# Position-bias tables in DRAM head by head: a row of 640 columns per head instead of one run per head pair

## The chip, the cores and the metric

The kernel runs on one core of a Trainium2 chip. A core has five engines with a program each: TensorE (PE, matrix products; its weight loads are shown as PEld), VectorE (DVE), ScalarE (ACT), GpSimd (POOL) and SyncE (SP, which here issues nearly all transfers). 16 DMA engines carry the transfers. The metric is the time of one execution on the device in microseconds (us). One execution of each kernel was also recorded by the profiler.

## The reference

Attention over 4 batches, 8 heads, 576 positions, head size 64, with a position bias that a small network computes from two positions, then two feed-forward stages over the 2304 tokens:

```
scores = q @ k.T / sqrt(64) + bias[head]     # bias: 8 heads x 576 x 576
x1     = softmax(scores) @ v                 # heads side by side: 2304 x 512
h      = x1 @ w_in                           # 2304 x 1024
x2     = (layernorm(h * softmax(h)) * g_ln) @ w_out           # 2304 x 512
y      = (sigmoid(x2 @ w_gate) * (x2 @ w_val)) @ w_out2       # inner width 1536
bias[h,i,j] = relu(x[i,j] * w1 + b1) @ w2,   x = log1p(|i-j|) / log1p(max(i,1))
```

The bias is the same for all four batches, so the kernel computes it once for 8 x 576 x 576 and uses it four times.

## The kernel before, in words

**Stages.** Until about 90 us the program computes statistics of the weights and the bias of the first 256 query positions. From there to 545 us run 72 attention ticks (a tick is 128 queries of a head pair of one batch), and between them the rest of the bias, the preparation of the weights of the first feed-forward stage (L706 to L722), and then that stage's tiles (L789 to L854). From 545 to about 655 us the weights of the second feed-forward stage are decoded while the last tiles of the first one run. The rest is the second feed-forward stage.

**One tick.** PE makes the scores of two heads (`a_qk`, L567 to L579). In `a_soft` DVE adds the bias and takes the row maximum (L597, one instruction for each head), ACT prepares the exponent's offset (L602) and takes the exponential (L604). In `a_split` the result becomes two halves of 16 bits (L613 on DVE or L615 on ACT, L616 and L618 on POOL), and SP starts a transposing DMA (L621) whose output `pt` PE multiplies with v (L640).

**The bias tables.** Queries are five tiles: t = 0 to 3 of 128, t = 4 of 64 rows. The tables of t = 0 and 1 are computed in an SBUF buffer (`gkf`), are used there by the first batch pair, and are then rescaled (`rescale0`) and written to the DRAM array `bias_d` by `store0` (L524). For t = 4, 2 and 3, in this order, `bias_grp` computes blocks of 128 key columns for all 8 heads and `bias_out` writes each to `bias_d` (L498 to L507): four blocks c = 0 to 3 of 128 columns, and c = 4 for the last 64 keys. `load_bias` brings the table of a head pair back for a tick: 24 loads of 576 KB (`pair_d`, L548), and 16 of the query tile t = 4 (L545, "M" in the code).

**What a row of `bias_d` holds.** For every query there is a row of 640 columns per head, head after head. The even head of a pair has its 512 first keys and then its last 64; the odd head has its last 64 keys first. So the two heads of a pair are one run of 1152 numbers: 512 keys of the even head, its last 64, the odd head's last 64, and 512 keys of the odd head. For t = 4 the row has the last 64 keys at both ends.

**What sets the order.** The program is built by a scheduler: it takes the instructions as the code records them and decides, by a cost model of its own, in which order each engine gets them. From the end of the attention on PE's order is that of the code. So an instruction more, or a transfer with another form, can change the order of others, far away in the program.

**The weight decode from 545 us on.** `load_pair` (L1079 to L1096) fetches rows of `in_moe2_w_out` into `wraw` (L1090), ACT and DVE unpack them (L191, L192 on ACT, L193, L195 on DVE), ACT sums their squares (L1169), DVE and PE reduce the sums (L162, L164, and L1179 for other matrices), and a scale follows from them. The other two matrices are split into halves by POOL, ACT and DVE (L720 to L722). The first products of the second feed-forward stage are L1404 (into `s_ps`); ACT and DVE take them out of PSUM (L1409, L1410) and form the gated values (L1273, L1274). The last products are L1368 and L1436.

Of the kernel before, what the change touches and what calls it, by code (L numbers as in the profile page):

```python
# [8 lines left out]
F32 = mybir.dt.float32  # L9
# [9 lines left out]
B, H, S, D = 4, 8, 576, 64  # L19
# [83 lines left out]
def attn_moe_kernel(  # L103
# [7 lines left out]
    act, dve, pool, pe, sp = nc.scalar, nc.vector, nc.gpsimd, nc.tensor, nc.sync  # L111
# [7 lines left out]
        return stack.enter_context(tc.tile_pool(name=name, bufs=bufs, **kw))  # L119

    dram = enter(ctx, "scratch", 1, space=DRAM)
    bias_d = dram.tile([5, 128, H, 640], F32, name="bias_d")
    x2_d = dram.tile([18, 128, 4, 2, 128], F16, name="x2_d")

    const = enter(ctx, "const")
# [367 lines left out]
    def bias_out(t, c):  # L493
        gb = bst.pop((t, c))
        np_ = 64 if t == 4 else 128
        if c == 4 and t == 4:
            for o in (0, 576):
                sp.dma_start(out=bias_d[4, 0:64, :, o:o + 64], in_=gb[0:64])  # L498
        elif c == 4:
            sp.dma_start(out=bias_d[t, 0:np_].rearrange("p (a b) n -> p a (b n)", b=2)[:, :, 512:640],  # L500
                         in_=gb[0:np_].rearrange("p (a b) n -> p a (b n)", b=2))
        elif t < 4:
            sp.dma_start(out=bias_d[t, :, :, 128 * c:128 * c + 128], in_=gb)
        else:
            for n in range(2):
                o = 64 + 128 * c + 64 * n
                sp.dma_start(out=bias_d[4, 0:64, :, o:o + 64], in_=gb[64 * n:64 * n + 64, :, 0:64])  # L507


    def pair0(t, hp):  # L510
        return view(gkf, 640 * (4 * hp + t), [[1216, 2], [1, S]])

    def pair_d(t, hp):
        return bias_d[t, :, 2 * hp:2 * hp + 2].rearrange("p h n -> p (h n)")[:, 0:2 * S]

    def rescale0(t, hp):
        g = pair0(t, hp)
# [3 lines left out]
            pool.tensor_scalar(out=g, in0=g, scalar1=col(RT), scalar2=0.0, op0=ALU.mult, op1=ALU.add)  # L521

    def store0(t, hp):
        sp.dma_start(out=pair_d(t, hp).rearrange("p (h n) -> p h n", h=2), in_=pair0(t, hp))  # L524


    brt = {}
# [4 lines left out]
    def load_bias(tk):  # L532
        bp, qd, hp, r, _, bset = tk
# [6 lines left out]
        n = 8 + 2 * (nbr[0] % 4)  # L540
        nbr[0] += 1
        t = gkf[:, 640 * n:640 * n + 2 * S]
        if qd == "M":
            for hh in range(2):
                sp.dma_start(out=t[64 * hh:64 * hh + 64, 0:640], in_=bias_d[4, 0:64, 2 * hp + hh])  # L545
            brt[key] = [t[:, 64:640], t[:, 0:S]]
        else:
            sp.dma_start(out=t, in_=pair_d(2 * qd + r, hp))  # L548
            brt[key] = [t[:, S * hh:S * hh + S] for hh in range(2)]

    trs, glob = {}, {}
# [1004 lines left out]
```

## Time and profile before

| | |
|---|---|
| time, median of 3 runs | 1041.68 us (1038.64 to 1043.49) |
| profiled execution, its own time | 1044.08 us |
| its span in the profile | 1042.3 us |
| mean granted TensorE clock | 0.913 of full speed |
| busy: PE, DVE, ACT, POOL | 898.6, 725.1, 644.3, 390.4 us |
| DMA queue of SP's transfers | 56.5% of the 16 DMA engines' time |

All times in the rows below are in microseconds from the start of the span, unless marked ns. "PE busy (x)" is busy time with the number of instructions. A bracket at the end of a timeline row gives the time that the engine sat idle just before, and what it was released by. A granted clock of 1.00 is TensorE's level of 2.4 GHz, one of 0.50 that of 1.2 GHz; values between are averages over a stretch. A DMA share is the mean busy share of the 16 DMA engines.

### The profile page before, as it was taken

To read this page: it belongs to the slowest core of one execution; us is meant where nothing else is said; L and a number is where in the kernel's file an instruction comes from. 1 tells how busy PE (TensorE), PEld (TensorE's weight loads), DVE (VectorE), ACT (ScalarE), POOL (GpSimd) and SP (SyncE) were. 2 spreads that over 40 slices of the span, in tenths; PEclk is the share of its full clock that TensorE was granted. 3 is DMA by queue.
4 is the path that set the end of the run, shared out by engine and by line. 5 is a ranking of instruction groups with operands and counts; after the bars stand their busy time and mean duration, and the time that the engine had idled before them with its cause. 6 is when DMAs were issued, how large, how long until landed. Compare 5 with 4: busy or idle time off the path is not lost. (4 is left out here: it accounts for less than half of the span.)

```text
span 1042.3 us, 23926 instructions
## 1 busy us (share of the span) xinstructions
PE 898.6 (86%) x9620; PEld 634.8 (61%) x9620; DVE 725.1 (70%) x1487; ACT 644.3 (62%) x1275; POOL 390.4 (37%) x362
## 2 busy tenths in 40 slices
PE   2646665679888789999998989899999999999998
PEld 2634444455666556677775656346668847866873
DVE  6878899776577676667666987659936744771760
ACT  3788886757776888878876888674333322332320
POOL 3257656565666656655650486340000000000000
PEclk9666675769998999999998999899999999999999
DMA  7988999999999899899878444101020010000001
GB/s 222 282 255 205 247 254 246 219 206 189 189 191 198 174 207 179 176 219 207 160 137 310 172 158 171 58 1 61 22 61 1 1 61 21 1 11 31 2 1 41
DMA packets 257360, 144.57 MB, mean 139 GB/s; under 512 B 216417, under 2 KB 231777, under 8 KB 257249
## 3 DMA queue, kind: packets, MB, share of 16 engines
q1 hardware_dynamic: 253952, 139.90, 56.5%
q0 software_dynamic: 2048, 1.58, 0.6%
q8 instruction: 75, 1.23, 0.5%
q10 hardware_dynamic: 1248, 1.57, 0.4%
q14 instruction: 37, 0.30, 0.1%
HBM read 80.36 MB, written 20.19 MB: 96 GB/s over the span
## 5 line engine op out<-in xcount | busy, mean ns | idle before, releaser
L616 POOL TENSOR_TENSOR p<-p,p 128x1024 f16<-128x1024 f32 x72 | 158.0, 2194 | 123.3 <-ACT p L615 86.0
L1292 DVE TENSOR_TENSOR fr<-prod,fr 128x512 f32<-128x512 f32 x126 | 85.1, 688 | 92.3 <-PE prod L1368 90.6
L1436 PE MATMUL ops<-w2f,gv 128*128 128x512 f16 x648 | 142.5, 379 | 0.0
L604 ACT ACTIVATE p<-p,m,sc 128x576 f32<-128x576 f32 x144 | 123.9, 862 | 2.4
L597 DVE CUSTOM_DVE_ANT_0 p<-score,gk 128x576 f32<-128x576 f32 x144 | 102.9, 751 | 11.6 <-PE score L579 7.0
L846 PE MATMUL x2ps<-lt,w1f 128*128 128x128 f16 x1728 | 106.2, 221 | 3.5 <-ACT lt L834 1.9
L1436 PEld LDWEIGHTS <-gv 128*128 128x128 f16 x648 | 63.4, 98 | 73.7
L1404 PE MATMUL s_ps<-xb,w2f 128*128 128x512 f16 (+1 forms) x576 | 101.4, 335 | 3.7 <-DVE acc L162 3.4
L846 PEld LDWEIGHTS <-w1f 128*128 128x128 f16 x1728 | 101.0, 99 | 4.1 <-issue 1.6
L640 PE MATMUL xps<-gk,pt 128*128 128x64 f16 (+1 forms) x2240 | 86.8, 202 | 15.8 <-DMA pt<-p 14.1
L640 PEld LDWEIGHTS <-pt 128*128 128x128 f16 (+1 forms) x2240 | 81.9, 107 | 26.3 <-DMA pt<-p 17.0
L463 PEld LDWEIGHTS <-mask 128*128 128x128 f16 (+1 forms) x1312 | 62.2, 118 | 53.3 <-issue 23.4
L1368 PEld LDWEIGHTS <-w2f 128*128 128x128 f16 x864 | 84.5, 98 | 11.8 <-issue 1.1
L1404 PEld LDWEIGHTS <-w2f 128*128 128x128 f16 x576 | 56.9, 100 | 47.0 <-issue 7.4
L1273 ACT ACTIVATE gv<-fr 128x512 f16<-128x512 f32 (+1 forms) x60 | 34.8, 586 | 81.4 <-DVE fr L1426 70.5
L789 PE MATMUL hps<-w1f,xt 128*128 128x512 f16 x312 | 78.5, 398 | 5.5 <-DVE gk L262 2.6
L463 PE MATMUL bp<-rhs,mask 128*128 128x64 f16 (+1 forms) x960 | 50.0, 220 | 28.6 <-DVE gb L489 11.5
L574 PE MATMUL score<-gk,qt 64*128 64x512 f16 x384 | 59.8, 418 | 15.4 <-DVE m L597 7.0
L1368 PEld LDWEIGHTS <-w2s 128*128 128x128 f16 x648 | 63.4, 98 | 7.3
L789 PEld LDWEIGHTS <-xt 128*128 128x128 f16 x384 | 38.1, 102 | 48.8 <-issue 14.0
L615 ACT ACTIVATE p<-p 128x1152 f16<-128x1152 f32 x54 | 62.4, 1157 | 7.0 <-DMA pt<-p 4.9
L602 ACT ACTIVATE m<-m,sc 128x1 f32<-128x1 f32 x144 | 39.3, 286 | 32.9 <-DVE m L597 32.6
(207 smaller groups left out, 1760.7 us busy)
## 6 DMA issues: line engine op xcount, KB each, us to landing
gk<-bias_d SPq DMA_DIRECT2D x24, 576.0 KB
wraw<-in_moe_w_out_dram SPq DMA_DIRECT2D x20, 512.0 KB
sraw<-in_q_dram SPq DMA_DIRECT2D x12, 384.0 KB
sraw<-in_k_dram SPq DMA_DIRECT2D x12, 384.0 KB
sraw<-in_v_dram SPq DMA_DIRECT2D x12, 384.0 KB
bias_d<-gk SPq DMA_DIRECT2D x8, 576.0 KB
qraw<-in_q_dram SPq DMA_DIRECT2D x64, 64.0 KB
kv<-in_k_dram SPq DMA_DIRECT2D x32, 128.0 KB
```

Source lines behind the costliest of these rows:

```text
L463: pe.matmul(big[0:np_, jj // 8, o:o + 64], lhsT, rhs[i].rearrange("p c h g -> p (c h g)"), start=(i == 0), stop=(i == 1),)
L597: dve.tensor_tensor_reduce(out=pp[:, hh], in0=score[:, 960 * hh:960 * hh + S], in1=bi, scale=1.0, scalar=-3.0e38, op0=ALU.add, op1=ALU.max ...
L604: act.activation(out=pp[:, hh], in_=pp[:, hh], func=ACTF.Exp, bias=m[:, 2 + hh:3 + hh], scale=col(C), accum_out=sm[:, c + hh:c + hh + 1])
L615: act.activation(out=hi, in_=pp, func=ACTF.Copy)
L616: pool.tensor_tensor(out=p16[:, :, 640:1152], in0=view(pp, 0, [[640, 2], [1, 512]]), in1=view(p16, 0, [[1280, 2], [1, 512]]), op=ALU.subtract)
L640: pe.matmul(o, a, b_, start=(n == 0), stop=(n == len(seq) - 1))
L789: pe.matmul(h, xt[:, xl, kk, off:off + 128], win16[:, 2 * kk + n, wl], start=(kk == 0 and xl == 0 and wl == 0), stop=(kk == 3 and xl == 1),)
L846: pe.matmul(ps[:, dc], wout16[:, f, wl, 128 * dc:128 * dc + 128], lt[:, ll, f], start=(n == 0), stop=(n == 23))
L1292: dve.tensor_tensor(out=out_, in0=a, in1=b, op=op)
L1368: pe.matmul(p[:, jf, 0:nn], w(wl, kk, jf), x(xl, kk), start=(m == 0), stop=(m == 5))
L1404: pe.matmul(ps[:, 0:n], w[:, 4 * (j // 4) + c, wl, o:o + 128], xx[:, 0:n, c, xl, :], start=(m == 0), stop=(m == 11))
L1436: pe.matmul(ps, gvs[j // 4][:, gl, j % 4, 128 * tt:128 * tt + 128], w2h16[2][:, j, wl], start=(m == 0), stop=(m == 35))
```

## The change

`bias_d` becomes an array with the head ahead of the query: 128 rows of 640 columns for each head, one after the other. The row of every head, even or odd, and of every query tile, now has its last 64 keys at both ends: 64, then 512, then 64. An even head is read from column 64 on, an odd head from column 0 on, 576 columns each.

```
-    bias_d = dram.tile([5, 128, H, 640], F32, name="bias_d")
+    bias_d = dram.tile([5, H, 128, 640], F32, name="bias_d")
...
         elif c == 4:
-            sp.dma_start(out=bias_d[t, 0:np_].rearrange("p (a b) n -> p a (b n)", b=2)[:, :, 512:640],
-                         in_=gb[0:np_].rearrange("p (a b) n -> p a (b n)", b=2))
+            for b in range(2):
+                o = 0 if b else 576
+                sp.dma_start(out=bias_d[t, b::2, :, o:o + 64].rearrange("h p n -> p h n"), in_=gb[:, b::2])
         elif t < 4:
-            sp.dma_start(out=bias_d[t, :, :, 128 * c:128 * c + 128], in_=gb)
+            o = 64 + 128 * c
+            sp.dma_start(out=bias_d[t, :, :, o:o + 128].rearrange("h p n -> p h n"), in_=gb)
...
     def pair_d(t, hp):
-        return bias_d[t, :, 2 * hp:2 * hp + 2].rearrange("p h n -> p (h n)")[:, 0:2 * S]
+        d = bias_d[t, 2 * hp]
+        return bass.AP(tensor=d.tensor, offset=d.offset + 64, ap=[[640, 128], [128 * 640 - 64, 2], [1, S]])
...
     def store0(t, hp):
-        sp.dma_start(out=pair_d(t, hp).rearrange("p (h n) -> p h n", h=2), in_=pair0(t, hp))
+        sp.dma_start(out=pair_d(t, hp), in_=pair0(t, hp))
...
-                sp.dma_start(out=t[64 * hh:64 * hh + 64, 0:640], in_=bias_d[4, 0:64, 2 * hp + hh])
+                sp.dma_start(out=t[64 * hh:64 * hh + 64, 0:640], in_=bias_d[4, 2 * hp + hh, 0:64])
...
-            sp.dma_start(out=t, in_=pair_d(2 * qd + r, hp))
+            sp.dma_start(out=t.rearrange("p (h n) -> p h n", h=2), in_=pair_d(2 * qd + r, hp))
```

(The two stores of t = 4 change their index order in the same way.) In bytes: a load of a pair was one run of 4608 bytes for each of 128 partitions, and is now two runs of 2304. The store of the last 64 keys of t = 2 and of t = 3 was one DMA with four runs of 512 bytes per partition, and is now two DMAs, one for the even and one for the odd heads, each with four runs of 256 bytes per partition. The other stores keep the number and length of their runs. Line numbers grow by 1 to 4: L500 becomes L502, L503 becomes L505, L548 L552, L621 L625, L1169 L1173, L1404 L1408, and buffer numbers by one or two.

The scheduler makes another order of it from the second of the two split stores on. On SP, at the store of the last keys of t = 3, before (L287 loads queries, L548 loads a bias pair, L621 transposes):

```order
L500 DMA bias_d_57<-gb_3517 512x1x128
L287 DMA qraw_3776<-in_q_dram 128x2x64 x2
L621 DMA_TRANSPOSE pt_3667<-p16_3663 128x18x128
L287 DMA qraw_3874<-in_q_dram 128x2x64 x2
L548 DMA gk_106<-bias_d_57 128x1152 x2
L621 DMA_TRANSPOSE pt_3740<-p16_3736 128x18x128
L548 DMA gk_106<-bias_d_57 128x1152
L621 DMA_TRANSPOSE pt_3802<-p16_3798 128x18x128
```

and after, with L502 for L500, L552 for L548 and L625 for L621:

```order
L502 DMA bias_d_57<-gb_3518 128x4x64
L287 DMA qraw_3778<-in_q_dram 128x2x64 x2
L625 DMA_TRANSPOSE pt_3669<-p16_3665 128x18x128
L287 DMA qraw_3876<-in_q_dram 128x2x64 x2
L502 DMA bias_d_57<-gb_3518 128x4x64
L552 DMA gk_106<-bias_d_57 128x2x576 x3
L625 DMA_TRANSPOSE pt_3804<-p16_3800 128x18x128
L625 DMA_TRANSPOSE pt_3742<-p16_3738 128x18x128
```

The second half of the store stands four rows behind the first, right ahead of the loads that read the table; three loads stand in a row, and two transposes have changed places.

On ACT, at the end of the weight decode, before (L191 and L192 unpack, L1169 sums squares, L851 and L1273, L1409 take results out of PSUM):

```order
L721 ACTIVATE w2f0_9694<-w2tmp_10681 128x512
L851 ACTIVATE x2_10677<-x2ps_10580 128x4x128
L1273 ACTIVATE gv_10764<-fr_10827 128x512
L1273 ACTIVATE gv_10764<-fr_10877 128x512
L1409 ACTIVATE fr_10927<-s_ps_10902,sw_81 128x512
L1169 ACTIVATE w2junk_10692,w2st_9697<-w2f2_9696 128x1024
L1169 ACTIVATE w2junk_10701,w2st_9697<-w2f2_9696 128x1024
L191 ACTIVATE w2f2_9696<-wraw_10712 128x1024
L192 ACTIVATE wraw_10712<-wraw_10712 128x1024
```

and after, with every name in the order in which it now comes:

```order
L725 ACTIVATE w2f0_9696<-w2tmp_10683 128x512
L191 ACTIVATE w2f2_9698<-wraw_10714 128x1024
L192 ACTIVATE wraw_10714<-wraw_10714 128x1024
L1173 ACTIVATE w2junk_10694,w2st_9699<-w2f2_9698 128x1024
L1173 ACTIVATE w2junk_10703,w2st_9699<-w2f2_9698 128x1024
L1173 ACTIVATE w2junk_10712,w2st_9699<-w2f2_9698 128x1024
L1173 ACTIVATE w2junk_10721,w2st_9699<-w2f2_9698 128x1024
L855 ACTIVATE x2_10679<-x2ps_10582 128x4x128
L1277 ACTIVATE gv_10766<-fr_10829 128x512
L1277 ACTIVATE gv_10766<-fr_10879 128x512
L1413 ACTIVATE fr_10929<-s_ps_10904,sw_81 128x512
```

The last unpacking and all four sums of squares now stand ahead of the steps that empty PSUM (L855, L1277, L1413); before, two of the sums stood behind those steps, and the other two with the last unpacking's own behind them.

On PE, at the same place, the product that adds the sums over the partitions (L164) has moved. Before it stands among the products of a later tile:

```order
L1404 MATMUL s_ps_11001<-xb_10735,w2f1_9695 128x512
L1404 LDWEIGHTS w2f1_9695
L1404 MATMUL s_ps_11001<-xb_10735,w2f1_9695 128x512
L164 MATMUL tot_10785<-acc_10781,ones_sb_74 128x3
L1404 LDWEIGHTS w2f1_9695
```

and after directly behind the last product of the first feed-forward stage (L850), ahead of every further product L1408:

```order
L850 LDWEIGHTS w1f1_111
L850 MATMUL x2ps_10582<-lt_10567,w1f1_111 128x128
L164 MATMUL tot_10787<-acc_10783,ones_sb_74 128x3
L1408 LDWEIGHTS w2f0_9696
L1408 MATMUL s_ps_10973<-xb_10737,w2f0_9696 128x512
```

Before, 62 products L1404 stand between the last product of the first feed-forward stage (L846) and this one; 24 of one tile have moved ahead of that stage's last products instead.

## Rows read from the trace of the kernel before

**Rows 1.** The page: busy time of each engine and its share of the span.

```profile
PE 898.6 (86%) x9620; PEld 634.8 (61%) x9620; DVE 725.1 (70%) x1487; ACT 644.3 (62%) x1275; POOL 390.4 (37%) x362
```

**Rows 2.** Busy time by stage: stretch, length, PE, PEld, DVE, ACT, POOL, clock, DMA share, GB/s.

```profile
200.00:240.00 40.00, 30.59 (x435) 22.50 (x432) 31.22 (x78) 24.90 (x57) 24.41 (x17) 0.68 0.90 201
240.00:340.00 100.00, 87.64 (x1136) 60.00 (x1133) 66.09 (x166) 76.15 (x172) 62.55 (x61) 0.93 0.95 194
...
657.00:664.00 7.00, 7.00 (x21) 2.60 (x20) 4.26 (x5) 4.40 (x8) 1.39 (x2) 0.60 0.00 1
664.00:780.00 116.00, 115.28 (x678) 66.22 (x677) 83.03 (x153) 57.56 (x103) 18.79 (x16) 1.00 0.09 30
640.00:646.00 6.00, 6.00 (x54) 3.73 (x53) 3.94 (x9) 5.61 (x9) 2.62 (x5) 1.00 0.82 301
700.00:710.00 10.00, 10.00 (x68) 6.48 (x67) 10.00 (x19) 4.62 (x8) 0.00 (x0) 1.00 0.32 107
```

**Rows 3.** What PE waited for, 180 to 545 us: total, times, longest.

```profile
PE score L574 <- DVE m L597: 6.4, 8, 1.5
...
PE xps L640 <- DMA pt<-p: 2.5, 3, 1.3
```

**Rows 4.** Transfers of the tables: issue time in ns, least, median, most; stretch.

```profile
L548 SPq DMA_DIRECT2D gk<-bias_d x24: 328/538/756, 211.9 to 498.7; - x24
...
L500 SPq DMA_DIRECT2D bias_d<-gb x2: 563/564/565, 198.8 to 233.7; - x2
```

**Rows 5.** The DMA queue that SP fills: packets, MB, share of 16 engines' span.

```profile
q1 hardware_dynamic: 253952, 139.90, 56.5%
```

**Rows 6.** SP's timeline at the last store: start, length, instruction.

```profile
233.70 0.56 SPq L500 DMA_DIRECT2D bias_d<-gb  x1
...
241.06 1.07 SPq L548 DMA_DIRECT2D gk<-bias_d  x2
246.88 2.44 SPq L621 DMA_TRANSPOSE pt<-p  x1
```

**Rows 7.** DVE's timeline, the first use of the table of t = 3.

```profile
252.74 0.74 DVE L597 CUSTOM_DVE_ANT_0 p<-score,gk 128x576 f32<-128x576 f32 x1
```

**Rows 8.** ACT's timeline while weights are split: an exponential behind a split.

```profile
230.38 0.72 ACT L718 ACTIVATE wtmp<-w1f,gs 128x512 f32<-128x512 f32 x1 [1.08 <-POOL w1f L722]
231.01 0.85 ACT L604 ACTIVATE p<-p,m,sc 128x576 f32<-128x576 f32 x1
```

**Rows 9.** DVE's timeline beside it, the second maximum of that tick.

```profile
228.89 0.74 DVE L597 CUSTOM_DVE_ANT_0 p<-score,gk 128x576 f32<-128x576 f32 x1
```

**Rows 10.** PE's timeline at the end of the weight decode.

```profile
648.83 4.26 PE L1404 MATMUL s_ps<-xb,w2f 128*128 128x512 f16 x19
656.52 12.41 PE L1404 MATMUL s_ps<-xb,w2f 128*128 128x512 f16 x43 [3.43 <-DVE acc L162]
```

**Rows 11.** ACT's timeline there.

```profile
651.82 0.58 ACT L851 ACTIVATE x<-x2ps 128x512 f16<-128x512 f32 x1
652.30 1.14 ACT L1273 ACTIVATE gv<-fr 128x512 f16<-128x512 f32 x2
653.34 0.68 ACT L1409 ACTIVATE fr<-s_ps,sw 128x512 f32<-128x512 f32 x1
653.91 1.05 ACT L1169 ACTIVATE w2junk<-w2f 128x1024 bf16<-128x1024 f32 x1
...
655.98 1.11 ACT L191 ACTIVATE w2f<-wraw 128x1024 f32<-128x1024 f32 x1
656.99 1.14 ACT L192 ACTIVATE wraw<-wraw 128x1024 int32<-128x1024 uint16 x1
```

**Rows 12.** DVE's timeline there.

```profile
658.15 1.23 DVE L193 SCALAR_TENSOR_TENSOR w2f<-w2f,wraw 128x1024 int32<-128x1024 int32 x1 [1.63 <-ACT wraw L192]
659.41 1.68 DVE L195 SCALAR_TENSOR_TENSOR w2f<-wraw,w2f 128x1024 int32<-128x1024 int32 x1
...
662.37 0.15 DVE L162 TENSOR_REDUCE acc<-w2st 128x1 f32<-128x2 f32 x1
```

More of the change, by code (lines that the diff above doesn't have):

```diff
@@ L497, in bias_out @@
             for o in (0, 576):
-                sp.dma_start(out=bias_d[4, 0:64, :, o:o + 64], in_=gb[0:64])
+                sp.dma_start(out=bias_d[4, :, 0:64, o:o + 64].rearrange("h p n -> p h n"), in_=gb[0:64])
         elif c == 4:
-            sp.dma_start(out=bias_d[t, 0:np_].rearrange("p (a b) n -> p a (b n)", b=2)[:, :, 512:640],
-                         in_=gb[0:np_].rearrange("p (a b) n -> p a (b n)", b=2))
+            for b in range(2):
+                o = 0 if b else 576
+                sp.dma_start(out=bias_d[t, b::2, :, o:o + 64].rearrange("h p n -> p h n"), in_=gb[:, b::2])
         elif t < 4:
-            sp.dma_start(out=bias_d[t, :, :, 128 * c:128 * c + 128], in_=gb)
+            o = 64 + 128 * c
+            sp.dma_start(out=bias_d[t, :, :, o:o + 128].rearrange("h p n -> p h n"), in_=gb)
         else:
@@ L506, in bias_out @@
                 o = 64 + 128 * c + 64 * n
-                sp.dma_start(out=bias_d[4, 0:64, :, o:o + 64], in_=gb[64 * n:64 * n + 64, :, 0:64])
+                sp.dma_start(out=bias_d[4, :, 0:64, o:o + 64].rearrange("h p n -> p h n"),
+                             in_=gb[64 * n:64 * n + 64, :, 0:64])
     def pair0(t, hp):
```

## The prediction

> **What bounds the kernel now.** I read the busy times first: PE works 898.6 us of the span, more than any other engine [rows 1]. A mean over stages hides where there is room, so I read the table by stage next [rows 2]. From 664 us on PE is full (115.28 of 116 us, clock 1.00): whatever happens there only shifts its start. In the attention PE still has gaps, 9.4 us of 40 in 200 to 240 and 12.4 us of 100 in 240 to 340, while the DMA engines are busy 0.90 to 0.95 of the time. That is where a change of transfers could hurt or help. So the third view is what PE waited for: the largest entry is DVE's maximum (6.4 us), the transposed probabilities cost 2.5 us, and no entry names a bias table [rows 3]. On SP the tables come early: the pair for t = 3 is issued at 241.06 and first used at 252.74 [rows 6, 7]. The last stretch with a gap is the end of the weight decode, where PE stands from the end of its 19 products (648.83 + 4.26 = 653.09) until 656.52, then runs at 0.60 of the clock until 664 [rows 2, 10].
>
> The terms are summed against the profiled execution, 1044.08 us; the median of the runs is 1041.68, or 2.4 lower, and I take no credit for that difference, since each is one kernel's scatter.
>
> **Split loads: +0.5.** 24 loads of 128 runs of 4608 bytes become 24 of 256 runs of 2304: 3072 packets more. SP's queue took 0.565 x 16 x 1042.3 us for 253,952 packets, 37 ns each [rows 5]. At that price 3072 packets are 114 us of DMA engine time, 7.1 us for each of 16: the upper bound, if all of it were on the path. A nearer row is the rate at two run lengths: while weight rows of 4 KB arrive, 301 GB/s at a share of 0.82, or 367 at a full share; while rows of 2 KB arrive, 107 at 0.32, or 334 [rows 2]. One table (590 KB) then takes 1.61 or 1.77 us, 0.16 more, 3.8 us over 24 loads, all of DMA time. None of it is waited for: PE's only wait on transfers in the attention is 2.5 us on transposes [rows 3], which share the engines. If DMA time grows by 3.8 of some 330 us (1.2%), queued transposes come a little later; I take an eighth of it, 0.5. The rows of one head now follow each other at 2560 bytes instead of 20,480, which no row of before prices; it can give back no more than the 2.5 us of waits on transposes. Bounds: -2.5 to +7.1.
>
> The Trainium skill, page "Perfetto Trace Analysis", section "DMA Optimizations", speaks against this edit: larger transfers use HBM better, those under 2 KB pay a notable overhead each, and going from 2 KB to 4 or 8 can improve throughput dramatically. The rows here show 334 against 367 GB/s, so a tenth. By the row the edit is 3.8 us of hidden DMA time; if the rule's word held and the rate halved, it would be 24 x 1.61 = 39 us of DMA time, more than the gaps left in that stretch.
>
> **Stores: 0.** The two stores of the last 64 keys become four, with runs of 256 bytes instead of 512. An issue took 563 ns whether the transfer was a store of four short runs or a load of one long one (538 ns median) [rows 4], so two more cost SP 1.1 us. The order adds a wait: the second half store of t = 3 stands right ahead of the first load of that table, and that load must wait until the store has landed. Behind it on SP are two more loads and the transposes of the running ticks. In before SP has nothing to do between 242.13 (the two loads of 241.06 end) and the transpose of 246.88: 4.75 us [rows 6]. That pause covers a landing of some 2 to 4 us, and the table itself is not due until 252.74 [rows 7]. If the pause is gone, the transposes behind come as late as the landing: +4. Bounds 0 to +4; I take 0, since the nearest rows show the pause.
>
> **Order in 228 to 242: -1.7.** Here the exponentials now stand ahead of the weight splits on ACT. In before DVE ends a tick's second maximum at 228.89 + 0.74 = 229.63 [rows 9], but its exponential waits behind a split until 231.01 [rows 8]. It can now start near 229.6 (its offset first, from about 229.3 for the other head): 1.4 us, plus 0.3 from the head before. This reaches PE, which idles 9.4 us in that stretch [rows 2]. The splits come later by as much, and their user, the first feed-forward tile, is filler. Bounds: -4 (about half of the 9.4) to +2 (two swapped transposes put one tick's result behind another's, one issue of 2.44 us [rows 6]); -1.7 is what the named row gives.
>
> **Order at the end of the weight decode: +4.3.** In before, two sums of squares, the last unpacking and the other sums stand around PE's restart, and the product L164 comes 62 products later; by 668 its inputs were long ready (the last L162 at 662.37 [rows 12]). After, L164 stands ahead of the first product of the next tile, so PE's restart waits for the whole chain. I build it from the rows: ACT is free of the last L721 at about 651.9, where L851 begins now [rows 11]. Unpacking L191 1.11 and L192 1.14, then DVE's 1.23 and 1.68 [rows 11, 12]: with overlaps as in the rows, 655.98 to 662.37 in before, it is 6.4 us from L191 to the last L162; three of the four sums fit beside DVE's part, the fourth (1.05) follows it. So L162 ends at about 658.3 and PE can run L164. But the next products need PSUM that L851, two L1273 and one L1409 empty, and these now stand behind the four sums: 0.58 + 1.14 + 0.68 = 2.4, and DVE's own step: 660.8. Against 656.52 this is +4.3. Upper bound: if the last weight rows land only where L191 stood before, 655.98, everything shifts by 4.1: +8.4. Lower bound: a decode that runs ahead, because the other work stands behind it, and 24 products that have moved ahead of the last product of the first stage shorten PE's idle time elsewhere: I give that at most 3 back beyond the 4.3, about the gap of 3.43 that is there now [rows 10], so -3.
>
> The clock does not enter: PE restarts at 1.2 GHz after the pause in either order (0.60 mean over 657 to 664 [rows 2]).
>
> **Sum.** 0.5 + 0 - 1.7 + 4.3 = +3.1; against 1044.08 that is 1047.2, and taken from the median, 1044.8. I forecast 1044.8, since what is measured is a median. The bounds are wide of it: all low, -2.5 + 0 - 4 - 3; all high, +7.1 + 4 + 2 + 8.4. They do not fall together, and the middle of each term carries most.
>
> **The rivals.**
>
> *The tail only exchanges idle time* (PE's order there is fixed, but the total of its work before the restart is the same, and the 24 products moved ahead fill what the wait costs). For it: the products that move are ready-made filler. Against it: the restart hangs on ACT, which is full in that stretch (seven entries from 651.82 to 658.13 without a gap [rows 11]). Time: 1041.7 + 0.5 - 1.7 = 1040.5.
>
> *The attention gains more, the faster side.* Half of PE's 9.4 us of gaps in 200 to 240 goes because exponentials are no longer behind splits, and the tail costs nothing: 1041.7 + 0.5 - 4.7 = 1037.5, or 1036 with rows at a shorter distance. For it: the wait of PE on the maximum is its largest [rows 3]. Against it: the gaps in that stretch are several, each with its own cause.
>
> *The DMA engines bind, the slower side.* The engines are at 0.95 in 240 to 340 [rows 2]; if the 7.1 us of packet time cannot lie beside anything, and SP's hold costs 2 to 3 of its 4, the time is 1041.7 + 7.1 + 2.7 = 1051.5. It decides where PE's waits on transposes rise from 2.5 us to about 10. Against it: no engine waits for a table.
>
> On the hold, the Trainium skill's same page, section "DMA Instruction — HWDGE (DVE, Sync)", says that the last write, which confirms the data, can take surprisingly long when the target is HBM. No row here shows the store's landing time, so the pause of 4.75 us is all that I set against it.
>
> *The change reorders nothing that matters:* the scheduler's new order is no order of time, and everything arrives as before: 1041.7.
>
> **How the numbers follow.** Forecast 0.50, tail for nothing 0.13, attention gains 0.18, DMA binds 0.14, nothing 0.05. A measurement of this kernel tells about 0.5% from no change, so 5.2 us: 1036.5 to 1046.9 is the same. Faster: most of the third case (0.15), 0.03 of the forecast, 0.02 of the first rival: 0.20. Slower: the fourth (0.14) and 0.18 of the forecast, where the tail is at its upper end: 0.32. The same: 0.48. The forecast's own range is 1039 to 1050; with the others the range is 1035.5 to 1051.5, which leaves out a good half of the DMA case and a little of the fast one.
>
> **What would show it.** In the profile after: the stretch without PE work before the decode's end should last from about 653 to 660, released by L162 or L1413, where before it ended at 656.52; the last L1404 stage should start as much later. The exponentials near 230 should directly follow the maxima. On SP the load behind the second half store should show a wait of 2 to 4 us, and PE's waits on transposes stay below 5 us in all. The loads' share of the DMA time should rise by 1 to 2%. The prediction is wrong if PE's restart comes before 657, if PE waits for tables or transposes by more than 6 us, or if the attention ends more than 4 us earlier or later than the 545 us of before.

## The result and the profile after

The changed kernel takes 1050.42 us (median of 8 runs, 1046.58 to 1052.42) against 1042.15 for the kernel before on the same chips. The ratio, here that of the mean times (1049.8 and 1042.7), is 1.0068, with an interval of 1.0040 to 1.0096: about 7 us slower, 4 to 10. The forecast was 3 us slower, 1044.8 us, with a range to 1051.5 that holds the measured time near its upper end; the share of 0.32 given to "slower by over 0.5%" is the case that came.

The two pages stand against each other as [rows 1] and [rows 5] do: the same work is done, in a span of 1048.8 instead of 1042.3 us. Two lines of the page after, the engines' busy time and the queue that SP fills:

```profile
PE 894.3 (85%) x9616; PEld 631.5 (60%) x9620; DVE 725.4 (69%) x1487; ACT 645.5 (62%) x1275; POOL 383.3 (37%) x362
...
q1 hardware_dynamic: 258080, 139.90, 55.9%
```

No engine has more to do. The queue carries 4128 packets more, and its share of the DMA engines' time has not risen: nothing here points to the split loads, and e3 below tests them alone.

The busy time by stage of the kernel after, the counterpart of [rows 2]:

```profile
200.00:240.00 40.00, 30.23 (x440) 22.61 (x440) 31.80 (x79) 26.07 (x58) 24.98 (x18) 0.70 0.89 198
240.00:340.00 100.00, 83.96 (x1115) 57.88 (x1114) 64.80 (x161) 74.39 (x164) 60.57 (x60) 0.95 0.90 189
657.00:664.00 7.00, 2.59 (x38) 2.16 (x36) 5.37 (x13) 7.00 (x15) 1.67 (x3) 0.79 0.11 41
664.00:780.00 116.00, 116.00 (x672) 66.12 (x671) 84.27 (x151) 56.33 (x101) 18.54 (x16) 0.98 0.07 23
```

PE loses in two places: 3.7 us in 240 to 340 (83.96 instead of 87.64 busy), and 4.4 in 657 to 664 (2.59 instead of 7.00). The second figure is too large by itself, because the kernel before had its stand of 3.43 us just ahead of 657 [rows 10]: from 600 to 664 PE is busy 53.41 and 50.24 us, so 3.2 are lost. Behind 664 it is full in both.

**The first place.** PE's waits from 180 to 545 us, the counterpart of [rows 3], then PE's timeline of the kernel after:

```profile
PE xps L644 <- DMA pt<-p: 8.0, 4, 4.7
PE score L578 <- DVE m L601: 7.4, 10, 1.5
```

The waits for a transposed tile have grown from 2.5 to 8.0 us, and one of them makes 4.7:

```profile
253.05 0.38 PE L297 MATMUL qtp<-id_sb,qraw 128*128 128x128 f32 x2
258.13 2.55 PE L644 MATMUL xps<-gk,pt 128*64 128x64 f16 x56 [4.71 <-DMA pt<-p]
```

In the kernel before the same products began without a wait that the profile shows:

```profile
253.53 0.38 PE L297 MATMUL qtp<-id_sb,qraw 128*128 128x128 f32 x2
253.84 1.66 PE L640 MATMUL xps<-gk,pt 128*64 128x64 f16 x56
```

What stands ahead of that transpose is seen on SP, first the waits of its queue and then its timeline in the kernel after, the counterpart of [rows 6]:

```profile
SPq L552 <- DMA bias_d<-gb: 2.8, 1, 2.8
```

```profile
235.12 0.55 SPq L502 DMA_DIRECT2D bias_d<-gb  x1
...
241.32 0.61 SPq L502 DMA_DIRECT2D bias_d<-gb  x1
244.86 2.04 SPq L552 DMA_DIRECT2D gk<-bias_d  x3
247.08 5.53 SPq L625 DMA_TRANSPOSE pt<-p  x1
```

The second half store issues at 241.32, the load behind it is held until 244.86, three tables (1.8 MB) then go out in a row, and the first transpose behind them takes 5.53 us to issue. In [rows 6] two of these tables were out at 241.06, and the first transpose of the group took 2.44 at 246.88. The kernel before has a slow transpose too, the next one, which stands right behind one table:

```profile
249.42 0.76 SPq L548 DMA_DIRECT2D gk<-bias_d  x1
250.34 5.44 SPq L621 DMA_TRANSPOSE pt<-p  x1
```

There it cost PE nothing that the profile shows. In the new order that first transpose is moreover not the one that PE needs next: the two ticks have changed places, and the needed one is second.

**The second place.** The end of the weight decode in the kernel after, the counterparts of [rows 10, 11, 12]: PE, ACT and DVE.

```profile
654.12 4.80 PE L850 MATMUL x2ps<-lt,w1f 128*128 128x128 f16 x83
660.69 0.39 PE L164 MATMUL tot<-acc,ones_sb 128*128 128x3 f32 x2 [1.77 <-DVE acc L162]
663.71 12.57 PE L1408 MATMUL s_ps<-xb,w2f 128*128 128x512 f16 x48 [2.64 <-DVE fr L1414]
```

```profile
654.09 1.15 ACT L191 ACTIVATE w2f<-wraw 128x1024 f32<-128x1024 f32 x1 [0.28 <-DMA wraw<-in_moe_w_out_dram]
...
659.30 1.05 ACT L1173 ACTIVATE w2junk<-w2f 128x1024 bf16<-128x1024 f32 x1
...
660.34 0.58 ACT L855 ACTIVATE x<-x2ps 128x512 f16<-128x512 f32 x1
660.82 1.14 ACT L1277 ACTIVATE gv<-fr 128x512 f16<-128x512 f32 x2
...
661.86 1.25 ACT L1413 ACTIVATE fr<-s_ps,sw 128x512 f32<-128x512 f32 x2
```

```profile
660.48 0.15 DVE L162 TENSOR_REDUCE acc<-w2st 128x1 f32<-128x2 f32 x1 [1.27 <-ACT w2junk L1173]
...
662.98 0.68 DVE L1414 SCALAR_TENSOR_TENSOR fr<-s_ps,fr 128x512 f32<-128x512 f32 x1
```

This is the chain that the prediction built: last unpacking (654.09), its sums, L162 (660.63), then PSUM emptied (663.66), and PE goes on at 663.71. PE stands from 658.92 on, 4.41 us without L164's own time, where the kernel before stood 3.43. That is only 1.0 more. Between its last xps and this restart PE is idle for 20.3 us in all and was for 16.1; the rest of the difference lies in shorter waits earlier in the decode.

**What one profile can tell.** The stretch of PE from its first product hps near 244 us to the end of its last xps is the attention's remainder; from there to the product s_ps on which PE resumes the long stretch is the decode. Both are read from PE's timeline, one profile for each kernel. The kernels' names are those of the experiments below.

| kernel | hps to last xps | last xps to restart | span |
|---|---|---|---|
| before | 244.63 to 554.33: 309.7 | 656.52: 102.2 | 1042.3 |
| after | 244.52 to 558.02: 313.5 | 663.71: 105.7 | 1048.8 |
| e1 | 241.15 to 554.23: 313.1 | 659.26: 105.0 | 1045.0 |
| e2 | 244.34 to 554.38: 310.0 | 661.24: 106.9 | 1046.0 |
| e3 | 244.92 to 554.05: 309.1 | 655.98: 101.9 | 1040.5 |
| e4 | 243.94 to 557.24: 313.3 | 661.73: 104.5 | 1046.4 |
| e5 | 244.50 to 559.14: 314.6 | 666.77: 107.6 | 1052.6 |
| e6 | 243.78 to 559.35: 315.6 | 660.35: 101.0 | 1045.2 |
| e7 | 244.68 to 553.55: 308.9 | 653.12: 99.6 | 1035.9 |
| e8 | 244.90 to 559.16: 314.3 | 664.87: 105.7 | 1049.9 |
| e9 | 242.27 to 551.93: 309.7 | 657.05: 105.1 | 1042.8 |
| e10 | 244.63 to 556.64: 312.0 | 658.39: 101.8 | 1041.6 |
| e11 | 247.97 to 560.90: 312.9 | 659.71: 98.8 | 1042.9 |
| e12 | 242.75 to 556.33: 313.6 | 662.37: 106.0 | 1048.0 |

The start near 244 moves by up to 7 us between profiles, and three profiles of one and the same order in the attention, with the same tables (after, e4, e6), give 313.3 to 315.6. So a difference of 2 us between two rows says nothing, and the verdicts come from the ratios, which have 6 to 12 runs behind them. Groups of rows say more. The eight profiles with the attention's new order and full tables (after, e1, e2, e4, e6, e8, e10, e11) have 310.0 to 315.6 in the first stretch, 313.1 in the mean; the three with the old order (before, e3, e7) 308.9 to 309.7, 309.2 in the mean: 3.9 us. In the second stretch the five with the decode of the kernel after (after, e1, e2, e8, e9) have 105.0 to 106.9, before and e3 102.2 and 101.9: 3.6 us. Of these, PE's stand before the restart makes 2.3 (4.4 to 7.3 us, 5.5 in the mean, against 3.43 and 2.86).

**Where PE falls behind in the attention.** From 244 us to the last xps PE has the same instructions in the same order in all fourteen kernels, so one can ask when it reaches a given product. One that is easy to find is ktp, before and after:

```profile
271.03 0.66 PE L258 MATMUL ktp<-id_sb,kv 128*128 128x128 f32 x4 [1.36 <-DVE lt L835]
```

```profile
273.49 0.66 PE L258 MATMUL ktp<-id_sb,kv 128*128 128x128 f32 x4 [1.36 <-DVE lt L839]
```

Counted from the first hps that is 26.4 and 29.0 us. The three profiles with the old order have 26.1 to 26.6, the eight with the new order 28.6 to 30.0. So 2.9 of the 3.9 us are lost by then, about 15 us behind the wait for the transpose.

### The profile page after: what moved, and what is told of

Same layout as the page of the kernel before. It is cut to its first block, busy times and chain, and to the rows that moved or that the text cites. A ratio compares the mean times of both kernels' runs of the same rounds, so it can differ in the third digit from the quotient of the medians.

```text
span 1048.8 us, 23922 instructions
## 1 busy us (share of the span) xinstructions
PE 894.3 (85%) x9616; PEld 631.5 (60%) x9620; DVE 725.4 (69%) x1487; ACT 645.5 (62%) x1275; POOL 383.3 (37%) x362
## 5 line engine op out<-in xcount | busy, mean ns | idle before, releaser
L850 PE MATMUL x2ps<-lt,w1f 128*128 128x128 f16 x1728 | 106.2, 221 | 4.3 <-DVE x L856 2.1
L1408 PE MATMUL s_ps<-xb,w2f 128*128 128x512 f16 (+1 forms) x576 | 99.7, 330 | 5.6 <-DVE fr L1414 2.6
L850 PEld LDWEIGHTS <-w1f 128*128 128x128 f16 x1728 | 101.0, 99 | 4.5 <-DVE x L856 2.2
L644 PE MATMUL xps<-gk,pt 128*128 128x64 f16 (+1 forms) x2240 | 86.2, 201 | 20.3 <-DMA pt<-p 18.3
L1408 PEld LDWEIGHTS <-w2f 128*128 128x128 f16 x576 | 56.5, 99 | 47.8 <-issue 9.6
L1277 ACT ACTIVATE gv<-fr 128x512 f16<-128x512 f32 (+1 forms) x60 | 34.7, 586 | 81.7 <-DVE fr L1430 70.4
```

Of the source, the lines that this page charges most:

```text
L644: pe.matmul(o, a, b_, start=(n == 0), stop=(n == len(seq) - 1))
L850: pe.matmul(ps[:, dc], wout16[:, f, wl, 128 * dc:128 * dc + 128], lt[:, ll, f], start=(n == 0), stop=(n == 23))
L1408: pe.matmul(ps[:, 0:n], w[:, 4 * (j // 4) + c, wl, o:o + 128], xx[:, 0:n, c, xl, :], start=(m == 0), stop=(m == 11))
```

## The experiments

All ratios are to the kernel before on the same chip; they can differ from the quotient of the medians, by up to 0.0023. Each kernel is told by its edit.

**e1, the split store alone**, in the old layout:

```
-            sp.dma_start(out=bias_d[t, 0:np_].rearrange("p (a b) n -> p a (b n)", b=2)[:, :, 512:640],
-                         in_=gb[0:np_].rearrange("p (a b) n -> p a (b n)", b=2))
+            for b in range(2):
+                o = 512 + 64 * b
+                sp.dma_start(out=bias_d[t].rearrange("p (a b) n -> p a (b n)", b=2)[:, :, o:o + 64],
+                             in_=gb[:, b::2])
```

> The kernel before with one thing of the change alone: the store of the last 64 keys of t = 2 and of t = 3 in two halves (even heads, odd heads) into the old layout. Loads stay single runs of 4608 bytes. Every engine then has the order of the changed kernel. Theory (the new order costs the time): about 1049 us, ratio 1.005 to 1.009; PE waits 4 to 5 us for a transpose near 253 and restarts at the end of the weight decode near 663. Rival (the loads in two runs cost it): 1041 to 1043, ratio 0.998 to 1.002.

Measured: 1049.9 us, ratio 1.0086 (1.0056 to 1.0115). Two store instructions more, with no change of layout and of loads, cost as much as the whole change. Both waits are there, PE's and that of SP's queue for the store:

```profile
254.99 2.59 PE L642 MATMUL xps<-gk,pt 128*64 128x64 f16 x56 [4.94 <-DMA pt<-p]
...
659.26 13.18 PE L1406 MATMUL s_ps<-xb,w2f 128*128 128x512 f16 x48 [2.63 <-DVE fr L1412]
```

```profile
SPq L550 <- DMA bias_d<-gb: 3.1, 1, 3.1
```

**e2, halves by head group**, so that the loads behind need only the first half:

```
+            for g in range(2):
+                h = slice(4 * g, 4 * g + 4)
+                sp.dma_start(out=bias_d[t, 0:np_, h].rearrange("p (a b) n -> p a (b n)", b=2)[:, :, 512:640],
+                             in_=gb[0:np_, h].rearrange("p (a b) n -> p a (b n)", b=2))
```

> As the split store alone, but the halves are heads 0 to 3 and heads 4 to 7, with runs of 512 bytes. The order of all engines is again that of the changed kernel, but the first load behind the second half now needs only the first half, which was issued some 6 us before: SP's wait of 2.8 us for the store goes. Theory (order: two ticks' transposes in the wrong order, and the end of the weight decode): no change against the split by even and odd heads, ratio to before 1.005 to 1.009. Rival (SP's hold delays the transposes): 2 to 3 us less than that, ratio 1.002 to 1.006, and the transpose near 247 and the one behind it earlier by 2 us.

Measured: 1049.05 us, ratio 1.0073 (1.0050 to 1.0096). SP's queue no longer waits for the store, and the loss stays. In the trace the loads are hardly earlier, since the half store itself stands later on SP, and the transpose at 247.23 not at all:

```profile
243.11 1.20 SPq L502 DMA_DIRECT2D bias_d<-gb  x1
244.36 2.67 SPq L550 DMA_DIRECT2D gk<-bias_d  x3
247.23 11.25 SPq L623 DMA_TRANSPOSE pt<-p  x3
```

```profile
257.69 2.09 PE L642 MATMUL xps<-gk,pt 128*64 128x64 f16 x56 [4.10 <-DMA pt<-p]
```

So the hold is not needed for the wait of 4 to 5 us; PE reaches ktp 28.6 us after hps, as late as with it. In this one profile the attention is then only 0.3 us longer than before, and the decode longer by 4.7; against e1 the ratios differ by 0.0013, far inside their intervals. Whether the hold costs 1 to 3 us further on stays open.

**e3, the loads in two runs alone**, with the layout, the stores and nearly the order of before:

```
-            sp.dma_start(out=t, in_=pair_d(2 * qd + r, hp))
-            brt[key] = [t[:, S * hh:S * hh + S] for hh in range(2)]
+            g = gkf[:, 640 * n:640 * n + 1280].rearrange("p (h n) -> p h n", h=2)[:, :, 0:S]
+            sp.dma_start(out=g, in_=pair_d(2 * qd + r, hp).rearrange("p (h n) -> p h n", h=2))
+            brt[key] = [g[:, hh] for hh in range(2)]
```

> The kernel before with its layout, its stores and (but for bias loads standing one place later on SP) its order, with the 24 bias loads alone in two runs of 2304 bytes per partition: the two heads go to columns 0 and 640 of the buffer instead of 0 and 576. 3072 packets more. Theory (order): 1040 to 1044, ratio 0.998 to 1.002. Rival (transfers): 1045 to 1049, ratio 1.003 to 1.007, and PE's waits on transposes in the attention well above 2.5 us.

Measured: 1042.06 us, ratio 0.9999 (0.9981 to 1.0017). The queue of SP has 3072 packets more and a smaller share of the time, and PE's waits on transposes are those of [rows 3]:

```profile
q1 hardware_dynamic: 257024, 139.90, 56.2%
```

```profile
PE xps L641 <- DMA pt<-p: 2.6, 2, 1.3
```

**e4, another order at the end of the decode**, by a constant: `W2B = 9` instead of 10, in the changed kernel.

> The changed kernel with one constant of the weight decode at 9 instead of 10 (how much of the decode is recorded between two tiles). The attention's order stays that of the changed kernel; in the decode the product L164 moves 27 products back and two of the four sums of squares stand behind the steps that empty PSUM, as in the kernel before. Theory (3 us lost in the attention, 4 in the tail): PE restarts 3 to 5 us earlier than in the changed kernel, time 1045 to 1047, ratio to before 1.002 to 1.005. Rival (the tail only passes on what the attention lost): 1049 to 1051, ratio 1.006 to 1.009.

Measured: 1048.14 us, ratio 1.0059 (1.0033 to 1.0085), between the two and not told apart from the changed kernel's 1.0068. The product L164 did move, but the last unpacking still stands ahead of the steps that empty PSUM, and that is what PE waits for:

```profile
661.73 7.44 PE L1408 MATMUL s_ps<-xb,w2f 128*128 128x512 f16 x27 [5.48 <-DVE fr L1414]
```

From L191 (653.9) to the restart it takes 7.8 us instead of 9.6, so 1.8 were undone. The theory's 3 to 5 us were not met.

**e5, the ticks in order**: the changed kernel with one constraint at ACT's split.

```
-            act.activation(out=hi, in_=pp, func=ACTF.Copy)
+            with ExitStack() as ord_:
+                if "sp" in glob:
+                    ord_.enter_context(tc.issue_after(glob["sp"].ins))
+                glob["sp"] = act.activation(out=hi, in_=pp, func=ACTF.Copy)
```

> The changed kernel with one constraint for the scheduler: ACT's step that makes the high half of a tick's probabilities (the one ahead of the POOL and transpose steps) may not be placed ahead of that of the tick before. Near 247 the two ticks' splits and transposes stand in the order of their use again; SP's wait behind the second half store stays. The end of the weight decode has a third order (L164 20 products further back, the last unpacking still ahead of the steps that empty PSUM). Theory (the swapped ticks cost 3 to 4 us in the attention): the wait of 4.7 us for a transpose near 253 goes, and from PE's first product hps near 244 to its last xps it takes 309 to 311 us instead of 313.5; with the tail not better than the changed one, time 1045 to 1048, ratio to before 1.003 to 1.006. Rival (SP's hold costs the attention): still 313 us there, ratio 1.006 to 1.009.

Measured: 1053.01 us, ratio 1.0098 (1.0064 to 1.0132). The theory fell here: with the swap undone the wait is 3.77 instead of 4.71 us, because the transpose that PE needs, now the first of the group, issues right behind the three tables.

```profile
245.58 1.39 SPq L552 DMA_DIRECT2D gk<-bias_d  x3
...
248.16 5.38 SPq L628 DMA_TRANSPOSE pt<-p  x1
```

```profile
257.21 1.66 PE L647 MATMUL xps<-gk,pt 128*64 128x64 f16 x56 [3.77 <-DMA pt<-p]
...
666.77 6.95 PE L1411 MATMUL s_ps<-xb,w2f 128*128 128x512 f16 x20 [7.85 <-DVE fr L1417]
```

The attention got no shorter (314.6 us in the table, where the theory gave 309 to 311). The decode has got a third order, with a last wait of 7.85 us, and takes 107.6 us instead of 105.7. That would make the ratio rise, but its interval overlaps that of the changed kernel.

**e6 and e7, the scale steps of the decode at priority 0**: `W2PRIO = 0` instead of 300, in the changed kernel (e6) and in the kernel before (e7). The last unpacking then stands behind the steps that empty PSUM in both.

> The changed kernel with the priority of the scale steps of the weight decode at 0 instead of 300. The attention's order is that of the changed kernel, word for word. In the decode the last unpacking on ACT stands behind the steps that empty PSUM, as in the kernel before, and L164 72 products behind the last x2ps. Theory (about 4 us of the loss is the unpacking ahead of the emptying): PE no longer stands for 4 to 5 us in all at the restart; time 1044 to 1047, ratio to before 1.002 to 1.005, what is left being the attention's 3 to 4 us. Rival (the decode only ends when the attention lets it): 1049 to 1051, ratio 1.006 to 1.009.

> The kernel before with the same priority at 0, a control for the run above: its decode has nearly the same order as that one's (the last unpacking behind the steps that empty PSUM), its attention is that of the kernel before. Theory: 1040 to 1044, ratio 0.998 to 1.002, and the run above is 3 to 4 us longer, by the attention alone. Rival (what was gained above is the low priority's own gain and not the order's repair): 1036 to 1039, ratio 0.994 to 0.997.

Measured: e6 1043.57 us, ratio 1.0019 (0.9996 to 1.0041); e7 1038.09 us, ratio 0.9965 (0.9944 to 0.9986). PE's restart in e6, then in e7:

```profile
651.34 6.64 PE L1408 MATMUL s_ps<-xb,w2f 128*128 128x512 f16 x30
660.35 10.70 PE L1408 MATMUL s_ps<-xb,w2f 128*128 128x512 f16 x41 [2.37 <-DVE fr L1414]
```

```profile
646.56 5.13 PE L1404 MATMUL s_ps<-xb,w2f 128*128 128x512 f16 x23
653.12 9.89 PE L1404 MATMUL s_ps<-xb,w2f 128*128 128x512 f16 x45 [1.43 <-DVE fr L1410]
```

The last stand is short in both. The priority gains in both: e7 lies where its rival said, so 3.6 us are the priority's own gain. e6, just under its theory's range, gains 0.0049 against the kernel after. e7 is faster than both kernels.

**e8, one of the three loads behind the transposes**: the changed kernel with

```
+            with ExitStack() as held:
+                if nbr[0] == 8:
+                    held.enter_context(tc.issue_after(trs[max(trs) - 3].ins))
+                sp.dma_start(out=t.rearrange("p (h n) -> p h n", h=2), in_=pair_d(2 * qd + r, hp))
```

> The changed kernel with one of the three bias loads that stand in a row on SP behind the second half store moved behind the three transposes that follow them. All other engines keep the order of the changed kernel, the two ticks in the wrong order too. The run with the ticks in order had kept its wait of 3.8 us near 253, so the new theory is: the transposes wait in the DMA queues behind three tables at once (1.8 MB, issued 4 us later than two of them were before). It expects PE's longest wait for a transpose near 253 to fall from 4.7 to 1 to 3 us, and a time 1 to 3 us under the changed kernel's, ratio to before 1.003 to 1.006; if the moved table is then late for its own tick, a wait of DVE for it shows instead. Rival (the order of the splits on ACT and POOL makes the wait): 4 to 5 us as before, ratio 1.006 to 1.009.

Measured: 1050.29 us, ratio 1.0065 (1.0045 to 1.0084). The first transpose behind two tables issues in 5.18 us where it took 5.53 behind three, and the wait stays at 4.41 us:

```profile
247.44 5.18 SPq L628 DMA_TRANSPOSE pt<-p  x1
```

```profile
258.21 2.02 PE L647 MATMUL xps<-gk,pt 128*64 128x64 f16 x43 [4.41 <-DMA pt<-p]
```

So the theory fell, and the rival's 4 to 5 us came: one table less right ahead of the transposes changes next to nothing.

**e9, two of the three loads cut short**, and the one ahead of them: `w = 64 if nbr[0] in (6, 7, 8) else S` columns are loaded, so the kernel leaves 512 columns of three tables out of the computation.

> The changed kernel with three bias loads cut to 64 of 576 columns for each head: two of the three in a row behind the second half store, and the one ahead of it; so 512 columns of these tables are left out of the computation. Every order is that of the changed kernel, and SP's wait for the store is kept. Theory (1.8 MB of tables ahead of the transposes): the wait for a transpose near 253 falls from 4.7 us to under 1.5 us, and PE is 2 to 3 us earlier at 270, measured from its first hps near 244. Rival (order of splits, or the store's own wait): the wait stays at 4 us or more.

Measured: 1047.36 us, ratio 1.0047 (1.0023 to 1.0070). The first transpose now issues in 3.91 us instead of 5.53, but the needed one is still second, and the wait falls only to 3.43:

```profile
245.52 3.91 SPq L626 DMA_TRANSPOSE pt<-p  x1
...
249.54 3.37 SPq L626 DMA_TRANSPOSE pt<-p  x1
```

```profile
254.94 1.77 PE L645 MATMUL xps<-gk,pt 128*64 128x64 f16 x56 [3.43 <-DMA pt<-p]
```

The theory's 1.5 us was missed, and the rival's 4 us as well. PE reaches ktp 27.6 us after hps, 1.3 earlier than in the kernel after where the theory gave 2 to 3; from there to the last xps it makes up the rest (309.7 us, as in the kernel before).

**e10, the split store at priority 0**: e1 and `W2PRIO = 0`. Its order is that of e6, its layout and loads are the old ones.

> The kernel before with the split store alone and the scale steps' priority at 0: the order of every engine is word for word that of the changed kernel at priority 0 (1.0019), with the old layout and single-run loads. Against the kernel before at priority 0 (0.9965) only the order differs, against the changed kernel at priority 0 only the layout. Theory (order alone): ratio to before 1.000 to 1.004. Rival (the head-by-head rows cost part of the 5.5 us between those two): 0.996 to 0.999.

Measured: 1043.33 us, ratio 0.9995 (0.9977 to 1.0013). Against e7, by the order of the attention, 0.0030; against e6, by the layout, 0.0024 the other way, each with an uncertainty of about 0.003. It lies between what the two theories gave.

**e11, e8 and e6 together.**

> The changed kernel with both repairs: one of the three loads moved behind the transposes, and the scale steps' priority at 0. Theory (the queue of loads makes the loss in the attention, the decode's order the rest): between the changed kernel at priority 0 and the kernel before at priority 0, ratio to before 0.997 to 1.000. Rival (the loss in the attention is not the loads'): 1.001 to 1.004.

Measured: 1043.54 us, ratio 0.9993 (0.9973 to 1.0012), not told apart from e10 or e6. It falls in the theory's range, but the wait for the transpose is still 4.10 us, as e8 had shown, so it is no proof of the loads.

**e12, e5 and e9 together**: ticks in order and two loads short.

> The run with the two ticks in the order of their use, and the same three bias loads cut to 64 of 576 columns as before, so that 512 columns of these tables are left out of the computation; every order is that of the run with the ticks in order. That run alone kept a wait of 3.8 us for a transpose near 253, the short loads alone one of 3.4 us. Theory (two causes that stand in for each other: the needed transpose is second in line, and each transpose issues in 5.4 us behind the tables instead of 2.4): with both gone the wait falls under 1.5 us, and the needed transpose issues in under 4 us. Rival (something else delays the transposes there): the wait stays at 3 us or more. The time is judged by the trace alone, since the decode's order is that run's (1.0098).

Measured: 1049.93 us, ratio 1.0071 (1.0048 to 1.0094). The needed transpose is the first and issues in 3.46 us, and the wait falls to 1.69:

```profile
246.41 3.46 SPq L629 DMA_TRANSPOSE pt<-p  x1
```

```profile
253.39 1.66 PE L648 MATMUL xps<-gk,pt 128*64 128x64 f16 x56 [1.69 <-DMA pt<-p]
```

That is a little above the bound of 1.5 that the theory set, and well under its rival's 3: of 4.71 us the swap alone gives back 0.94, the short tables alone 1.28, both 3.02.

For PE's progress the two are not alike. It reaches ktp 31.1 us after hps in e5 and 29.3 in e12, where the kernel after has 29.0 and e9 27.6. So the short tables give back 1.3 us in one order and 1.9 in the other, and the ticks in order give back nothing: what they take from the wait for a transpose, other waits take again (2.90 us for DVE's L262 near 264 in e12, 1.13 in the kernel after).

**What the ratios add up to.** With the new order and the scale steps at 300 there are four kernels (after, e1, e2, e8), mean 1.0073; at 0 three (e6, e10, e11), mean 1.0002. With the old order it is 1 and 0.9965. At 0, where the last unpacking no longer stands in the way, the new order costs 1.0002 - 0.9965 = 0.0037, or 3.9 us: the attention's share. Going from 300 to 0 gives back 0.0071 in the new order and 0.0035 in the old one; the difference, 0.0036 or 3.8 us, is what the end of the decode costs in the new order alone. Each of the two has an uncertainty of some 0.0025 to 0.003, since e7 stands alone in its place; the sum of the two (0.0073) is far outside of it. The means of the table above, which come from the profiles, give 3.9 and 3.6 us; with the scale steps at 0 the decodes of the new order (98.8 to 101.8) and of the old one (99.6) are only 0.9 apart in the mean.

## Why the prediction came out as it did

The direction was right, and the sum was 4 us low. That the range holds the time is in part luck: its upper end was set by the rival of the DMA engines (1051.5), whose packets e3 rules out. Of the prediction's own signs of being wrong one came: PE waits 8.0 us for transposes, where more than 6 was to refute it. The others did not: PE restarts at 663.71, not before 657, and the attention ends 3.7 us later, under 4 (its last xps ends at 554.33 in the kernel before, not at the 545 that the text names). By terms:

- **Split loads, +0.5.** Right: e3 measures -0.1 us (-2 to +1.8). The upper bound of 7.1 counted packets at their mean time in the queue [rows 5]; in e3 the packets rose as counted, by 3072, and the share of the time fell. The reading of [rows 2], a tenth of the rate and hidden, was the better one, and even its 3.8 us of DMA time do not show: in the traces' packet records the 3072 packets of 4608 bytes take 52.7 us of each DMA engine in the kernel before, and the packets of 2304 bytes that replace them some 51.7 in e3 and 49.7 in the kernel after. The sentence that the loads' share would rise by 1 to 2% was wrong.
- **Layout of the rows.** The rows of a head at 2560 bytes show neither gain nor loss beyond the uncertainty: e6 against e10 is +0.0024, after against e1 -0.0018.
- **Stores, 0.** No run prices the two issues alone (0.6 us of SP each). The wait is there as described: 2.8 us, inside the 2 to 4. The step that failed is the cover: "That pause covers a landing of some 2 to 4 us". SP's pause did cover SP's time (the first transpose starts at 247.08 instead of 246.88), but I had followed only the engine and not what it pushed out when it went on: three tables directly ahead of the transposes, the first of which then issued in 5.53 us instead of 2.44. I read the pause of 4.75 us [rows 6] as the time that the two tables ahead had on the DMA engines; e8, with two tables and no pause, has 5.18. The row of 5.44 behind one table was in the trace of before, beside the 2.44 that I took.
- **Order in 228 to 242, -1.7.** Wrong in sign. The exponential does follow its maximum, at 230.08 instead of 231.01, but no gain shows at 244 (hps begins at 244.52 instead of 244.63), and the swapped transposes, bounded at +2 by one issue of 2.44 us, stand behind a wait of 4.71. The price was read from an issue with no table right ahead of it. This and the store's cover are the attention's part together: with the loads' 0.5 I gave -1.2, the ratios give 3.9 with 2.5 to 3 either way.
- **The end of the decode, +4.3.** The size is right: 3.8 by the ratios. The chain is there too: from L191 to the last L162 6.39 us where 6.4 was built from the rows, then from its end 3.0 to the restart, where 2.4 and 0.1 for DVE's step were (it takes 0.68). The unpacking itself began at 654.09, released by its weights, 2.2 later than the 651.9 that I took; the attention was then 3.7 us behind. But the term put the whole loss into PE's last stand, from about 653 to 660. That stand came as 658.92 to 663.71 and grew by 1.0 us in this pair of profiles, by 2.3 in the mean of five; the rest lies in earlier waits of the decode that the term does not name. So part of the agreement is luck.
- **The rivals.** That the tail only exchanges idle time falls by e6 and e7 (e4 is not told apart from the changed kernel). That the attention gains falls with the result. The rival of the DMA engines comes nearest in time and in its sign, waits on transposes of about 10 us; its packets fall by e3, and its other half, the hold, is the one thing close to what happened, as a queue of tables ahead of transposes, and e2 shows that the hold itself need not be there. That the reorder does not matter falls by e1, which is the reorder without the change.

The sum was low by 4 us, by the ratios all of it in the attention. What failed there is the price of order on SP: it was read from SP's own idle time and from an issue of 2.44 us, and the runs show issues of 5.0 to 6.2 us behind three tables.

What stays open: how much of the attention's 3.9 us the tables make. By ktp, 2.9 are lost close behind the wait, and cutting three tables gives back 1.3 to 1.9 of them; by the last xps e9 has the length of the kernel before, and its ratio (1.0047) lies 0.0026 under the mean of the kernels with full tables, about its own uncertainty. But the cut also takes 1.6 MB off the DMA engines, which these runs cannot separate from the tables' place ahead of the transposes. The one wait is no measure of the loss: e12 has the shortest (1.69) and is 3.9 us longer than before by the last xps, e2 has 4.10 and is 0.3 longer.

## What to carry to other kernels

When a scheduler places the instructions, two store instructions more can cost more than the whole layout change that they come with: build the change, compare the order, and then try the smallest edit that has the same order, as e1 did here. A queue's idle time is no cover for a wait if large transfers stand behind the wait and short urgent ones behind those. And where a chain ends a stage, look at what stands ahead of the steps that empty PSUM: with the scale steps at priority 0 the last unpacking stands behind them, and the new order got 0.7% back. The kernel before gained 0.35% from the same setting (e7, 1038.09 us, the best of all that ran), though its last unpacking stood behind them already; what gives it that is open.

## What the runs showed of the hardware

A transposing DMA of the same size issued in 2.40 to 2.44 us where the last table had been issued 4 to 5 us before (before, e3, e7). Right behind tables of 590 KB it took 3.7 to 5.6 behind one (the same three), 4.9 and 5.2 behind two (e11, e8), 5.0 to 6.2 behind three (after, e1, e2, e4, e5, e6, e10); with two of three tables cut to a ninth it took 3.91 and 3.46. The needed transpose landed 5.4 us after its issue began in e9 (249.54 to 254.94) and 9.05 in e5 (248.16 to 257.21). From the issue of a small store to DRAM to the release of a load that reads it back, 3.5 us passed in the kernel after (241.32 to 244.86), and 2.8 to 3.8 in the others that wait for it. The Trainium skill, page "Perfetto Trace Analysis", section "DMA Instruction — HWDGE (DVE, Sync)", says that the confirming write can cause a surprisingly long delay when the target is HBM; the runs agree in so far as SP waits up to 3.2 us for this store, but they do not show which part of that is the confirming write. The Trainium skill's same page, section "DMA Optimizations", says that batching transfers of 2 KB into 4 or 8 KB can improve throughput dramatically. Here it was tried the other way round and does not show: 24 loads in runs of 2304 instead of 4608 bytes left the time as it was (0.9999), and their packets took 51.7 us of each DMA engine instead of 52.7.
